# Attention in blocks: rows read and normed half a block earlier, and the sums of queries, keys and values queued from the middle of the block before

## The chip, the cores and the metric

The kernel runs on one core of one Trainium2 chip. The metric is the device time of one execution in microseconds (us), the median of several executions. Three executions before the change gave a median of 2226.68 us (2222.89 to 2229.94).

## What is computed

Two layers, one after the other, on x of 2048 rows and 640 columns. Each layer is a Fourier mixing (two matrix products along the hidden size, two along the rows) and then an attention in a sliding window of 256 rows with 32 heads of 20 columns, each behind a layer norm and each added to its input:

```
x = x + _A_ref(_layernorm(x), dft_seq_re, dft_seq_im, dft_hid_re, dft_hid_im)
x = x + _B_ref(_layernorm(x), wqkv, wo)
...
def _B_ref(x, wqkv, wo):
    H = 32; Dh = D // H; W = 256
    q, k, v = (x @ wqkv), split by heads
    scores = q k^T * Dh ** -0.5
    mask = (idx[:, None] - idx[None, :] >= 0) & (idx[:, None] - idx[None, :] < W)
    p = softmax(where(mask, scores, -1e9))
    return (p v) @ wo
```

## The kernel before

Every matrix product of two float32 operands is made as three float16 products (high x high, high x low, low x high) into one sum. The mixing stage of a layer ends with the input of the attention in DRAM (`x2_d`), 16 tiles of 128 rows. The first two tiles (block 0) are normed and turned at the end of the mixing stage; all other rows are read, normed and turned inside the attention.

**Blocks, visits, steps.** `attention` walks through 8 blocks of 256 rows. A block takes 16 visits; `now[0]` counts them in twos, so that a block runs over the steps r = 0, 2, ... 30, and "r18 of block 4" is a place in the program. A visit deals with four heads and 128 queries: `scores` (query times key, for the row maxima), 8 visits later `by_key` (the same products, turned) and `probabilities`, 11 later `values`, 12 later `back`. Per visit VectorE runs L1133 twice and L1134 twice, GpSimd runs L1188 and L1190, ScalarE L1184 twice.

**Fill.** Behind these, a visit runs one unit of fill on TensorE, mostly 15 matmuls: a sum of queries or keys (`qk`, 10 units per block: 5 of keys, then 5 of queries), of values (`v`, 4 units), or of the output projection (`out`, 4 units). `next_unit` takes the ready unit that is due first; `must` prefers those that the coming block needs, from a point that MUST_TO and FIRST_TO set. At r0 of block b, `queue_qk(b + 1)` and `queue_v(b + 1)` put the units of the next block into the fill, the sums due at r24 (QK_SLOT). `flush` forces what is left.

**From a sum to the scores.** A sum goes to `qf` (ScalarE L361) and to high and low parts in `early` (GpSimd L362, L363), and is stored to DRAM (`qkd<-early`). The store is held for one visit (`hold`). When the last of 5 sums is through, `load_stack` loads the block's keys (`ks<-qkd`) or queries (`qs<-qkd`) with six DMAs into the form that the heads need, and `ones_stack` fills the rows beside them. There are two buffers of queries and three of keys, so that the loads of block b + 1 can't start before r16 of block b (the `at` of `hold`). The row maxima go to DRAM and back (`htd<-ht`, `qs<-htd`, four visits ahead of their use).

**Rows.** At r26 of block b two tiles of block b + 3 are read from `x2_d` (L185, `x<-x2d`), at r0 of the next block `rows_norm` starts: its parts run as `slow_step`s, one or two per visit, on VectorE (L138, L141, L147 to L151, L165), then `split` on ScalarE (L176) and GpSimd (L177). `rows_turn` turns the result with a DMA transpose (L193, `early<-xs`), in layer 0 at r18, in layer 1 at r26, and marks the rows as done 6 steps later; the sums of the block wait for that mark. `new_rows`, at r14, takes the buffer for them (two in turn).

**Queues.** All these DMAs are issued by SyncE, in the order of the program (`load`, L185; `turn_load`, L193), with those of the output projection: `ot<-os` (a transpose), `x<-x2d` and `x3d<-x`. A DMA whose data isn't ready holds up all behind it. TensorE, VectorE, ScalarE and GpSimd also run in the order of the program; all matmuls are issued by L125.

Of the kernel before, what the change touches and what calls it, by code (L numbers as in the profile page):

```python
# [12 lines left out]
F16 = mybir.dt.float16  # L13
# [5 lines left out]
S, D, H, DH, P = 2048, 640, 32, 20, 128  # L19
NT = S // P  # L20
ND = D // P
# [4 lines left out]
NP = H // 2  # L26
# [8 lines left out]
FULL_TO = 244  # L35
FIRST_FILL = 2000
FILL_LAST = 8
QK_SLOT = 24
NEXT_STEPS = (10, 22)
OUT_STEPS = (4, 40, 8)  # L40
LAST_STEPS = (1, 258)
# [2 lines left out]
KEY_LAG = 8  # L44
VALUE_LAG = 11
BACK_LAG = 12
STEPS = ((1, 2), (0, 2))
MUST_TO = 24
HOLD = 2
FIRST_TO = 4  # L50
PIECES = 2
TURN_LAG = 6
UNIT = 384
# [1 line left out]
M_UP = 2.0 ** 15  # L55
SHIFT = -20.0
TURN_STEPS = 8
X2_STEP = 26
ROWS_STEP = 14
HIDDEN_STEP = 10  # L60
ROW_STEPS = 3
# [10 lines left out]
def body(ctx: ExitStack, tc: tile.TileContext, x_in, cmat, whid, wqkv, wo, out):  # L72
    nc = tc.nc
    pers = ctx.enter_context(tc.tile_pool(name="pers", bufs=1))
    keep = ctx.enter_context(tc.tile_pool(name="keep", bufs=1))
# [733 lines left out]
    def attention(layer, proj, dst, final):  # L809
        with ExitStack() as st:  # L810
# [6 lines left out]
            sb = pool("sb")  # L817
# [5 lines left out]
            fill = []  # L823
# [12 lines left out]

            def proj_qk(b, w, ct):
                if ct == 0:
                    hold(partial(ones_stack, b, w), 2 * NP * (b - 1) + 2 * KEY_LAG if b > 2 else 0)
                yield from proj.qk(b, w, ct)  # L840
                if ct == ND - 1:
                    hold(partial(load_stack, b, w), 2 * NP * (b - 1) + 2 * KEY_LAG if b > 2 else 0)

            def proj_v(b, ti, n):
                j = 2 * b + ti
# [79 lines left out]
            held = []  # L925

            def hold(f, at=0):
                held.append((max(now[0] + HOLD, at), f))

            def run_held(upto):  # L930
                for item in [h for h in held if h[0] <= upto]:
                    held.remove(item)
                    item[1]()

            proj.held = hold
            slow, idle, handed, later = deque(), deque(), deque(), []

            def new_xs():
                while len(later) > 2:
                    later.pop(0)[1]()  # L940
                return sb.tile([P, 2, D], F16, tag="xs", name="xs", bufs=3)

            def run_later():
                while later and later[0][0] <= now[0]:
                    later.pop(0)[1]()

# [16 lines left out]
            def split_wo():  # L963

                fs = [keep.tile([P, D], F32, tag="res1", name="wst", bufs=2) for n in range(2)]
                for n in range(2):
                    load(fs[n], wo[:, n])
                yield
                for n in range(ND):
                    f, sc = fs.pop(0), wsc[:, 1:2]  # L970
                    nc.scalar.activation(bo[0][:, n], f, AF.Copy, scale=sc)
                    nc.vector.scalar_tensor_tensor(bo[1][:, n], f, sc, bo[0][:, n], op0=OP.mult, op1=OP.subtract)
                    for _ in range(3):
                        yield
                    if n + 2 < ND:
                        fs.append(keep.tile([P, D], F32, tag="res1", name="wst", bufs=2))
                        load(fs[-1], wo[:, n + 2])

            def rows_norm(b, x2s):

                ys = []
                yield from norm_steps(x2s, ys)
                for t, y in enumerate(ys):
                    xs = new_xs()
                    split(xs[:, 0], xs[:, 1], y, nc.gpsimd)
                    later.append((now[0] + ROW_STEPS, partial(rows_turn, b, xs, t)))
                    yield

            def rows_turn(b, xs, t):
# [16 lines left out]
            OS, OT, X2, done = {}, {}, {}, {}  # L1006
# [3 lines left out]
            now = [0]  # L1010
# [75 lines left out]
            def flush(kind):  # L1086
                while any(u.kind == kind for u in fill) or (unit[0] and unit[0].kind == kind):
                    if unit[0] is None:
                        unit[0] = min((u for u in fill if u.kind == kind), key=lambda u: u.due)
                        fill.remove(unit[0])  # L1090
                    if step(unit[0]) is None:
                        unit[0] = None
                if kind[0] == "qk":
                    run_held(1 << 20)

            TOP, PT, topped = {}, {}, [None]

# [120 lines left out]
            def back(n):  # L1218
                b, k = divmod(n, NP // 2)
                t = PVS.pop(n)  # L1220
                pv = new_f().rearrange("p (a b) -> p a b", a=4)
                for m in range(2):
                    transpose(pv[:, 2 + m], t[:, m], idf)
                pbv = pv[:, 2:].rearrange("p m (h e) -> p (m h) e", e=32)
                if k == 0:
                    flush(("out", b - 3))
                    OS[b] = sb.tile([P, 2, 2, D], F16, tag="os", name="os", bufs=3)
                r = sb.tile([P, 8], F32, tag="r", name="r", bufs=2)
                cs = slice(4 * k * DH, 4 * (k + 1) * DH)
                o = sb.tile([P, 2, 4 * DH], F32, tag="o", name="o", bufs=2)  # L1230
                hi, lo = (OS[b][:, :, m, cs] for m in range(2))
                nc.vector.reciprocal(r, pbv[:, :, DH])
                nc.vector.tensor_tensor(o.rearrange("p m (h e) -> p (m h) e", e=DH), pbv[:, :, :DH],  # L1233
                                        r.unsqueeze(2).to_broadcast([P, 8, DH]), op=OP.mult)
                nc.gpsimd.tensor_copy(hi, o)  # L1235
                nc.gpsimd.tensor_tensor(lo, o, hi, op=OP.subtract)
                last = b == NBQ - 1
                d1 = (k + 1) * 4 * DH // P
                if last and d1 > k * 4 * DH // P and (d1 > 2 or k > LAST_FROM):
                    for m in range(2):  # L1240
                        step0 = max(now[0] + LAST_STEPS[0], NG + 2 * KEY_LAG if m else LAST_STEPS[1] if d1 < ND else 0)
                        fill.append(Unit(step0, last_out(2 * b + m, lastd[0], d1), "last", NS + 2 * d1 + m, [(2 * b + m - 2, 2)]))
                    lastd[0] = d1
                elif k == NP // 2 - 1 and not last:
                    for m in range(2):
                        i = 2 * b + m
                        at, due, kind = now[0] + OUT_STEPS[0] + OUT_STEPS[2] * m, 2 * NP * (b + 2) + OUT_STEPS[1], ("out", b)
                        need = [(i - 2, 2)] if i > 1 else []
                        outs.append((at, need, partial(out_turn, i)))
                        fill.append(Unit(at, out_tile(i), kind, due + 3 * m + 2, [(i, 1)]))  # L1250

            NBQ = S // QB

            NG = NT * NP
            NS = NG - 4 + 2 * BACK_LAG

            def queue_qk(b):
                for w in (1, 0):
                    for ct in range(ND):
                        need = [("rows", b, t) for t in range(2)] if b > 1 else []  # L1260
                        fill.append(Unit(0, proj_qk(b, w, ct), ("qk", b), 2 * NP * (b - 1) + QK_SLOT, need, ns=15 * 109))

            def queue_v(b):
                for ti in range(2):
                    for n in range(2):
                        fill.append(Unit(2 * NP * (b - 1), proj_v(b, ti, n), ("v", b), 2 * NP * b + 2 * VALUE_LAG, ns=15 * 136))

            def slow_step():
                with tc.issue_after(topped[0]):
# [17 lines left out]
            for G in range(NS // 2 + 1):  # L1287
                now[0] = g = 2 * G
                b, r = divmod(g, 2 * NP)
                if g < NG:  # L1290
                    if r == 0:
                        flush(("qk", b))
                        if b < NBQ - 1:
                            queue_qk(b + 1)
                            queue_v(b + 1)
                    scores(G)
                keyed = 0 <= G - KEY_LAG < NG // 2
                if keyed:
# [13 lines left out]
                n = due(G, BACK_LAG)  # L1312
                if n is not None:
                    back(n)
                c = b + 2 + (r > 0)
                if g < NG and c < NBQ and (g == 0 or r == X2_STEP):
                    x2s = [keep.tile([P, D], F32, tag="res0", name="x2", bufs=2) for t in range(2)]
                    for t in range(2):
                        load(x2s[t], x2_d[2 * c + t])
                if g < NG and c < NBQ and r == 0:  # L1320
                    slow.append(rows_norm(c, x2s))
                if g < NG and r == ROWS_STEP:
                    flush(("v", b))
                    if b < NBQ - 2:
                        proj.new_rows(b + 2)
                if g < NG and r == HIDDEN_STEP:
                    if b == NBQ - 1 and not final:
                        flush(("v", b))
                        hidden = Hidden(xu_d)
                        pieces = hidden.pieces()  # L1330
                        for k in range(2):
                            fill.append(Unit(g + NEXT_STEPS[k], hidden.stage(k, None), "next", NG + k))
# [4 lines left out]
                    next(pieces, None)  # L1337
                while handed and handed[0][0] <= now[0]:
                    handed.popleft()[1]()
                run_held(now[0])  # L1340
                if outs and outs[0][0] <= g and all(k in done for k in outs[0][1]):
                    outs.pop(0)[2]()
                n = due(G, VALUE_LAG)
# [46 lines left out]
```

## Time and profile before

| | us |
|---|---|
| median of three executions | 2226.68 |
| the profiled execution | 2233.76 |
| its span in the trace | 2232.0 |
| TensorE busy, all stages | 2038.7 |
| first mixing stage, 0 to 578.2 | 578.2 |
| attention of layer 0, blocks 0 to 7, 578.2 to 1097.8 | 519.6 |
| attention of layer 1, blocks 0 to 7, 1668.0 to 2181.8 | 513.8 |

The span is that of the one profiled execution, from its first to its last instruction; 1.8 us of its time lie outside. In the prediction, rows of stretches give the stretch in microseconds from the span's start, its length, and per engine (PE, PE's weight loads, VectorE, ScalarE, GpSimd) the busy time with the number of instructions, then the clock that TensorE was granted (1.00 is full), the DMA share and GB/s. Rows of a timeline give start, time, engine, line, operation, operands and, in brackets, the idle time ahead and what ended it; "SPq" is SyncE's queue.

### The profile page before, as it was taken

The page shows a single profiled execution, that of the slowest core. Times are in us where ns is not written, and L with a number is a line of the kernel's source. Part 1 is how long each engine was busy: PE and PEld are TensorE (multiplying, and loading weights), DVE is VectorE, ACT ScalarE, POOL GpSimd, SP SyncE. Part 2 cuts the span into 40 slices and gives each one's busy share as a digit, 9 for nine tenths or more (in the row PEclk, how much of TensorE's full clock was granted, in tenths as well). Part 3 has the DMA queues.
Part 4 walks back from the last instruction along what each step waited for, and adds up shares of the span by engine and source line. Part 5 has one row for each costly group of instructions (what it writes and reads, how often), then busy time and mean ns, then how long its engine had stood idle before and what let it go on. Part 6 is the DMA issues. An engine that isn't in the chain of part 4 may idle for free.

```text
span 2232.0 us, 54291 instructions
## 1 busy us (share of the span) xinstructions
PE 2038.7 (91%) x21145; PEld 1470.8 (66%) x21145; DVE 1507.8 (68%) x3253; ACT 1127.5 (51%) x1971; POOL 1448.6 (65%) x2170
## 2 busy tenths in 40 slices
PE   7999999999988998899889999999998899988987
PEld 4667666767656776666556777677675676766764
DVE  8777778676676776655538677775857676755652
ACT  5444455433255666555554444343424566655654
POOL 5667688769455777655457768676755676656643
PEclk9999999999999999999999999999999999999989
DMA  7555565474534555434436454545754334434321
GB/s 252 179 199 178 181 213 197 146 281 150 127 81 110 108 114 104 89 80 106 137 115 182 146 185 149 166 168 186 256 142 85 88 81 104 110 83 105 79 63 49
DMA packets 280502, 311.00 MB, mean 139 GB/s; under 512 B 107572, under 2 KB 214836, under 8 KB 271156
## 3 DMA queue, kind: packets, MB, share of 16 engines
q1 hardware_dynamic: 279668, 306.88, 47.3%
q8 instruction: 165, 2.70, 0.5%
q14 instruction: 93, 0.76, 0.1%
q10 hardware_dynamic: 576, 0.66, 0.1%
HBM read 201.72 MB, written 83.46 MB: 128 GB/s over the span
## 4 chain that ended last, share of the span: by engine, by line
PE 57%; DVE 16%; DMA 11%; ACT 5%; issue 4%; POOL 3%; SPq 3%; DVEq 0%; POOLq 0%; ACTq 0%
PE pf L125 26%; PE y L125 10%; PE st L125 7%; PE x L125 7%; PE z L125 6%; DVE cc L523 5%; DMA qs<-qkd 4%; DVE m L1134 3%; ACT ptq L1184 3%; SPq L185 2%; DVE st L1133 2%; DMA qkd<-early 2%; DMA ks<-qkd 2%; DMA res<-accd 1%; DVE lnt L150 1%
## 5 line engine op out<-in xcount | busy, mean ns | idle before, releaser
L125 PEld LDWEIGHTS <-cc 128*128 128x128 f16 x5376 | 525.2, 98 | 209.1 <-issue 8.2
L1184 ACT ACTIVATE ptq<-st,shift,alpha 128x768 f32<-128x768 f32 (+2 forms) x512 | 484.7, 950 | 305.8 <-PE st L125 253.0
L125 PEld LDWEIGHTS <-big 128*128 128x128 f16 x4320 | 417.9, 98 | 164.3 <-issue 62.2
L1133 DVE COPY_PREDICATED st<-mask,st 128x256 f32<-128x256 int32 x448 | 190.0, 424 | 251.9 <-PE st L125 247.3
L1134 DVE TENSOR_REDUCE m<-st 128x2 f32<-128x512 f32 (+1 forms) x512 | 342.5, 671 | 10.7 <-DVE st L1133 0.5
L125 PE MATMUL pf<-early,big 128*128 128x256 f16 x2400 | 289.8, 274 | 7.9 <-ACT ht L1151 4.3
L125 PE MATMUL pf<-big 128*128 128x320 f16 x1680 | 242.0, 302 | 28.3 <-DVE zc L283 16.7
L125 PE MATMUL y<-zc,cc 128*128 128x320 f16 x1728 | 263.4, 299 | 3.7 <-DVE pf L546 3.7
L1188 POOL TENSOR_SCALAR_AFFINE_SELECT ptq<-ptq 128x512 f32<-128x512 f32 x224 | 145.8, 651 | 155.5 <-ACT ptq L1184 155.1
L523 DVE SCALAR_TENSOR_TENSOR cc<-cs,cc 128x512 f16<-128x512 f32 x256 | 229.0, 901 | 0.0
L520 ACT ACTIVATE cc<-cs 128x512 f16<-128x512 f32 x256 | 149.1, 621 | 135.1 <-POOL cs L513 61.1
L125 PE MATMUL st<-ks,qs 62*128 62x128 f16 (+1 forms) x2016 | 131.3, 240 | 83.5 <-DMA qs<-qkd 43.7
L523 DVE SCALAR_TENSOR_TENSOR cc<-cq,cc 128x512 f16<-128x512 f32 x192 | 198.6, 1035 | 0.2 <-ACT cc L520 0.2
L1190 POOL TENSOR_SCALAR_AFFINE_SELECT ptq<-ptq 128x512 f32<-128x512 f32 x256 | 164.3, 642 | 47.0 <-ACT ptq L1184 46.4
L125 PE MATMUL pf<-ptq,v 128*32 128x128 f32 (+1 forms) x3840 | 188.2, 335 | 1.6 <-DVE early L283 1.2
L125 PEld LDWEIGHTS <-qs 62*128 62x128 f16 x2016 | 85.1, 95 | 144.3 <-issue 123.6
L125 PE MATMUL z<-zc,cc 128*128 128x320 f16 x1152 | 177.7, 299 | 2.7 <-DVE res L546 1.7
L125 PE MATMUL x<-zc,cc 128*128 128x320 f16 x1152 | 178.9, 300 | 0.0
L587 POOL TENSOR_TENSOR res<-res,pf 128x320 f32<-128x320 f32 x64 | 77.7, 1214 | 138.8 <-DVE pf L546 130.7
L1235 POOL CAST os<-o 128x160 f16<-128x160 f32 x128 | 41.8, 326 | 183.3 <-DVE o L1233 183.2
L125 PE MATMUL pf<-big,early 128*128 128x320 f16 x960 | 149.6, 311 | 1.7 <-ACT ht L1151 0.9
L125 PEld LDWEIGHTS pf<-ptq,v 128*32 128x32 f32 x3840 | 112.6, 111 | 44.1 <-issue 3.5
(135 smaller groups left out, 3364.5 us busy)
## 6 DMA issues: line engine op xcount, KB each, us to landing
cq<-in_cmat_dram SPq DMA_DIRECT2D x64, 1024.0 KB
accd<-res SPq DMA_DIRECT2D x96, 320.0 KB
res<-accd SPq DMA_DIRECT2D x96, 320.0 KB
x<-x2d SPq DMA_DIRECT2D x64, 320.0 KB
qkd<-early SPq DMA_DIRECT2D x160, 128.0 KB
ks<-qkd SPq DMA_DIRECT2D x108, 160.0 KB
qs<-qkd SPq DMA_DIRECT2D x84, 160.0 KB
x2d<-res SPq DMA_DIRECT2D x32, 320.0 KB
```

The source lines that it names most:

```text
L125: i = getattr(nc.tensor, what)(*args, **kw)
L150: ts(u, g, g, h, op0=OP.mult, op1=OP.mult)
L185: i = nc.sync.dma_start(out, in_)
L520: nc.scalar.activation(cc[m][:, 0], f, AF.Copy, scale=C_UP)
L523: nc.vector.scalar_tensor_tensor(cc[m][:, 1], f, C_UP, cc[m][:, 0], op0=OP.mult, op1=OP.subtract)
L587: nc.gpsimd.tensor_tensor(x1[:, hi], x1[:, hi], p1, op=OP.add)
L1133: nc.vector.copy_predicated(sp[:, :, 2 * P:3 * P], mask[:, None, :].to_broadcast([P, 2, P]), far)
L1134: topped[0] = nc.vector.tensor_reduce(TOP[n][:, pi, :, k], sp[:, :, c0:3 * P], axis=AX.X, op=OP.max).ins
L1184: nc.scalar.activation(o[:, pi], tps[pi][:, :, first * P:3 * P], AF.Sigmoid, bias=shift, scale=alpha[:, 0:1])
L1188: nc.gpsimd.affine_select(out=q[:, :, a0], in_=q[:, :, a0], pattern=[[0, 4], [-1, P]], base=0, channel_multiplier=1, compare_op=OP.is_gt, ...
L1190: ins = nc.gpsimd.affine_select(out=q[:, :, a0 + 2], in_=q[:, :, a0 + 2], pattern=[[0, 4], [1, P]], base=0, channel_multiplier=-1, compare ...
L1235: nc.gpsimd.tensor_copy(hi, o)
```

## The change

- `queue_qk` and `queue_v` of block b + 2 are called at r14 of block b (ROWS_STEP), behind `new_rows`; block 0 alone still queues block 1 at r0. Units of values now also wait for their rows. The sums are due at r20 (QK_SLOT, MUST_TO).
- The rows of block b + 3 are read at r12 (X2_STEP) and their norm starts at r16 of block b. `rows_turn` waits in a list of its own (`turning`) until r16 of the next block, in tiles of their own (`rx`, two); the tile `xs` of `next_norm` comes from the pool `keep`, two in turn.
- The loads of queries and keys keep their earliest place (`at`), for block 2 too; `flush` no longer runs held DMAs ahead of it, and the run at the end of a visit takes those whose time has come.
- The output units of layer 0 wait until the weights `wo` are split.

```diff
-QK_SLOT = 24
+QK_SLOT = 20
-MUST_TO = 24
+MUST_TO = 20
-FIRST_TO = 4
+FIRST_TO = 0
-X2_STEP = 26
+X2_STEP = 12
...
-                    hold(partial(ones_stack, b, w), 2 * NP * (b - 1) + 2 * KEY_LAG if b > 2 else 0)
+                    hold(partial(ones_stack, b, w), 2 * NP * (b - 1) + 2 * KEY_LAG if b > 1 else 0)
...
-                    hold(partial(load_stack, b, w), 2 * NP * (b - 1) + 2 * KEY_LAG if b > 2 else 0)
+                    hold(partial(load_stack, b, w), 2 * NP * (b - 1) + 2 * KEY_LAG if b > 1 else 0)
...
-                held.append((max(now[0] + HOLD, at), f))
+                held.append((max(now[0] + HOLD, at), f, at))
...
-                for item in [h for h in held if h[0] <= upto]:
+                for item in [h for h in held if min(h[0], max(h[2], upto)) <= now[0]]:
...
-                while len(later) > 2:
+                while len(later) > 1:
                     later.pop(0)[1]()
-                return sb.tile([P, 2, D], F16, tag="xs", name="xs", bufs=3)
+                return keep.tile([P, 2, D], F16, tag="xs", name="xs", bufs=2)
...
+                while turning and turning[0][0] <= now[0]:
+                    turning.pop(0)[1]()
...
+                    if n == ND - 1:
+                        done["wo"] = now[0]
...
-                    xs = new_xs()
+                    xs = sb.tile([P, 2, D], F16, tag="rx", name="rx", bufs=2)
                     split(xs[:, 0], xs[:, 1], y, nc.gpsimd)
-                    later.append((now[0] + ROW_STEPS, partial(rows_turn, b, xs, t)))
+                    turning.append((max(now[0] + ROW_STEPS, 2 * NP * (b - 2) + ROWS_STEP + 1), partial(rows_turn, b, xs, t)))
...
-                    run_held(1 << 20)
+                    run_held(0)
...
-                        fill.append(Unit(at, out_tile(i), kind, due + 3 * m + 2, [(i, 1)]))
+                        fill.append(Unit(at, out_tile(i), kind, due + 3 * m + 2, [(i, 1)] + ["wo"] * (layer == 0)))
...
-                        fill.append(Unit(2 * NP * (b - 1), proj_v(b, ti, n), ("v", b), 2 * NP * b + 2 * VALUE_LAG, ns=15 * 136))
+                        need = [("rows", b, ti)] if b > 1 else []
+                        fill.append(Unit(2 * NP * (b - 1), proj_v(b, ti, n), ("v", b), 2 * NP * b + 2 * VALUE_LAG, need, ns=15 * 136))
...
                     if r == 0:
                         flush(("qk", b))
-                        if b < NBQ - 1:
-                            queue_qk(b + 1)
-                            queue_v(b + 1)
+                        if b == 0:
+                            queue_qk(1)
+                            queue_v(1)
...
-                c = b + 2 + (r > 0)
+                c = 2 if g == 0 else b + 3
...
-                if g < NG and c < NBQ and r == 0:
+                if g < NG and c < NBQ and (g == 0 or r == X2_STEP + 4):
                     slow.append(rows_norm(c, x2s))
                 if g < NG and r == ROWS_STEP:
                     flush(("v", b))
                     if b < NBQ - 2:
                         proj.new_rows(b + 2)
+                        queue_qk(b + 2)
+                        queue_v(b + 2)
...
-                run_held(now[0])
+                run_held(1 << 20)
```

Two places show how instructions move. The first is SyncE in layer 0, the later half of block 4. `qkd_0_157` are the queries of block 5, `qkd_1_158` its keys, `x2d_93` and `x2d_94` the rows of block 7, `ot<-os` a transpose for the output projection, `htd` the row maxima. Before:

```order
L193 DMA_TRANSPOSE ot<-os 128x10x128
L185 DMA x_12108<-x2d_84 128x640
L185 DMA xud_129<-xs 128x1280
L185 DMA qs<-htd_163 2x512 x2
L185 DMA qkd_0_157<-early 128x2x256
L185 DMA htd_164<-ht 16x128
L185 DMA x_12252<-x2d_93 128x640
L185 DMA x_12253<-x2d_94 128x640
L185 DMA qkd_0_157<-early 128x2x256
L185 DMA qs<-qkd_0_157 20x16x256 x6
```

The same place after the change:

```order
L193 DMA_TRANSPOSE early<-rx 128x10x128 x2
L185 DMA qs<-htd_165 2x512 x2
L185 DMA ks<-onesd_169 2x4096 x2
L185 DMA ks<-qkd_1_158 20x16x256 x6
L185 DMA qs<-onesd_168 2x4096 x2
L185 DMA qkd_0_157<-early 128x2x256
L185 DMA htd_166<-ht 16x128
L185 DMA qkd_0_157<-early 128x2x256
L185 DMA res<-x3d_95 128x640
L185 DMA qs<-htd_166 2x512 x2
L185 DMA qkd_0_157<-early 128x2x256
L185 DMA qs<-qkd_0_157 20x16x256 x6
```

The output transpose and the two reads of rows no longer stand between the last stores and the load of the queries; the transposes of rows (`early<-rx`) now stand ahead of the keys' load, and the queries' load follows it within a few rows.

The second is VectorE in layer 0, where the norm of block 7's rows starts. `x_12252` and `x_11774` are the tile of these rows, before and after; L916 is the second half of an output tile. Before:

```order
L916 SCALAR_TENSOR_TENSOR x_12108<-pf,beta,x_12108 128x320
L1133 COPY_PREDICATED st_6968<-mask,st_6968 128x2x128
L1232 RECIPROCAL r<-pf 128x8
L1134 TENSOR_REDUCE m<-st_6968 128x2
L1133 COPY_PREDICATED st_6969<-mask,st_6969 128x2x128
L1233 TENSOR_TENSOR o<-pf,r 128x160
L1134 TENSOR_REDUCE m<-st_6969 128x2
L138 BN_STATS lnst<-x_12252 128x6
```

After:

```order
L1137 COPY_PREDICATED st_6968<-mask,st_6968 128x2x128
L1236 RECIPROCAL r<-pf 128x8
L1138 TENSOR_REDUCE m<-st_6968 128x2
L1137 COPY_PREDICATED st_6969<-mask,st_6969 128x2x128
L1237 TENSOR_TENSOR o<-pf,r 128x160
L1138 TENSOR_REDUCE m<-st_6969 128x2
L138 BN_STATS lnst<-x_11775 128x6
L916 SCALAR_TENSOR_TENSOR x_10644<-pf,beta,x_10644 128x320
```

The statistics of these rows move from the first visit of block 5, behind output tile 5 (`x_12108`), to the middle of block 4, ahead of the end of output tile 3 (`x_10644`); lines from L976 on have numbers higher by 2 to 7 in the changed kernel (L1133 is L1137 there, L1232 is L1236).

More of the change, by code (lines that the diff above doesn't have):

```diff
@@ L935, in attention @@
             proj.held = hold
-            slow, idle, handed, later = deque(), deque(), deque(), []
+            slow, idle, handed, later, turning = deque(), deque(), deque(), [], []
             def new_xs():
-                while len(later) > 2:
+                while len(later) > 1:
                     later.pop(0)[1]()
-                return sb.tile([P, 2, D], F16, tag="xs", name="xs", bufs=3)
+                return keep.tile([P, 2, D], F16, tag="xs", name="xs", bufs=2)
             def run_later():
+                while turning and turning[0][0] <= now[0]:
+                    turning.pop(0)[1]()
                 while later and later[0][0] <= now[0]:
```

## The prediction

> **What bounds the kernel now.** I read the chain of waits first: it tells which engine sets the end.
>
> ```profile
> PE 57%; DVE 16%; DMA 11%; ACT 5%; issue 4%; POOL 3%; SPq 3%; DVEq 0%; POOLq 0%; ACTq 0%
> PE pf L125 26%; PE y L125 10%; PE st L125 7%; PE x L125 7%; PE z L125 6%; DVE cc L523 5%; DMA qs<-qkd 4%; DVE m L1134 3%; ACT ptq L1184 3%; SPq L185 2%; DVE st L1133 2%; DMA qkd<-early 2%; DMA ks<-qkd 2%; DMA res<-accd 1%; DVE lnt L150 1%
> ```
>
> TensorE (PE) carries the end, but 4% stands on `qs<-qkd`, the load of a block's queries, and 2% on `qkd<-early`, the store of their sums. Both belong to attention, so I cut the two attention stages into their blocks. Every 32nd L1133 (two per visit, 16 visits per block) opens a block. Columns: stretch, length, busy time of each engine with its instructions, granted clock, DMA share, GB/s. The rows are blocks 1 to 6, of layer 0 and then of layer 1.
>
> ```profile
> 635.30:702.80 67.50, 55.62 (x723) 40.29 (x724) 44.38 (x108) 37.44 (x66) 39.90 (x86) 0.93 0.40 89
> 702.80:763.90 61.10, 58.32 (x857) 43.54 (x857) 49.40 (x126) 41.58 (x64) 45.20 (x99) 1.00 0.46 88
> 763.90:825.30 61.40, 58.62 (x858) 43.69 (x859) 49.73 (x126) 41.09 (x63) 45.26 (x99) 1.00 0.54 124
> 825.30:899.10 73.80, 59.24 (x857) 44.07 (x857) 47.48 (x120) 42.31 (x65) 46.45 (x100) 0.94 0.50 108
> 899.10:968.50 69.40, 64.34 (x888) 47.11 (x889) 45.01 (x109) 41.51 (x64) 43.61 (x98) 0.97 0.44 100
> 968.50:1036.50 68.00, 63.38 (x887) 46.80 (x887) 38.30 (x85) 40.37 (x62) 40.42 (x92) 0.98 0.34 80
> ...
> 1720.70:1788.20 67.50, 57.55 (x722) 40.88 (x723) 43.47 (x105) 36.34 (x64) 38.74 (x86) 0.91 0.41 89
> 1788.20:1847.80 59.60, 57.81 (x857) 43.36 (x857) 44.45 (x107) 40.95 (x63) 43.71 (x98) 1.00 0.39 85
> 1847.80:1914.10 66.30, 59.74 (x857) 44.32 (x858) 44.99 (x108) 40.52 (x62) 43.75 (x98) 0.97 0.48 106
> 1914.10:1982.90 68.80, 58.88 (x857) 43.96 (x858) 44.55 (x107) 40.84 (x63) 43.64 (x98) 0.95 0.50 113
> 1982.90:2054.90 72.00, 63.90 (x888) 47.32 (x888) 44.98 (x109) 41.49 (x64) 43.70 (x98) 0.95 0.40 86
> 2054.90:2124.90 70.00, 63.63 (x887) 47.19 (x888) 38.30 (x85) 40.38 (x62) 40.40 (x92) 0.96 0.35 78
> ```
>
> These rows carry the argument. Blocks of 857 matmuls do the same work, and last from 59.6 to 73.8 us. The shortest, block 2 of layer 1, has a clock of 1.00 and PE busy for 57.81 of its 59.60 us. So an undisturbed visit takes 59.6 / 16 = 3.73 us, and what a block has beyond that is a stall, or the lower clock around one. The waits of PE name the stalls: over 578.2 to 1097.8 us (layer 0) and then 1668 to 2182 us (layer 1); total, times, longest.
>
> ```profile
> PE st L125 <- DMA qs<-qkd: 20.4, 7, 8.4
> PE pf L125 <- DMA ot<-os: 5.4, 1, 5.4
> ```
>
> ```profile
> PE st L125 <- DMA qs<-qkd: 23.2, 8, 4.7
> PE pf L125 <- DMA early<-xs: 3.9, 2, 3.1
> PE pf L125 <- DMA ot<-os: 2.7, 1, 2.7
> ```
>
> Fifteen waits for a block's queries, 43.6 us. The longest shows how they come about: SyncE's queue in layer 0, block 4 (start, issue time), and then PE.
>
> ```profile
> 862.49 2.87 SPq L185 DMA_DIRECT2D ks<-qkd  x6
> ...
> 870.68 4.50 SPq L193 DMA_TRANSPOSE early<-xs  x2
> ...
> 884.93 0.38 SPq L185 DMA_DIRECT2D qkd<-early  x1
> 888.58 2.90 SPq L185 DMA_DIRECT2D qs<-qkd  x6
> ```
>
> ```profile
> 894.40 0.37 PE L125 MATMUL st<-ks,qs 62*128 62x256 f16 x1 [8.36 <-DMA qs<-qkd]
> 897.63 0.71 PE L125 MATMUL st<-ks,qs 62*128 62x256 f16 x8 [2.87 <-DMA qs<-qkd]
> ```
>
> SyncE issues in program order. The last store of sums left at 884.93, the load had to wait for it until 888.58, and PE, through with block 4, stood for 8.36 + 2.87 us. The query sums of block 5 end at step r24 of block 4 and their load stands at r26: three visits (11.2 us) before the block's end, for store, load and whatever SyncE has ahead of them.
>
> **The change part by part.** *Sums earlier.* The sums of block b+2 enter the fill at r14 of block b instead of r0 of block b+1. In the new order of the program a block's query sums end at r18 or r20, and the load stands at r20 or r22 (before: sums at r20 to r24, load at r22 to r26). Against the stalls: in layer 0 the load into block 5 goes from r26 to r20, three visits or 11.2 us, against a wait of 11.2 us; in layer 1 from r26 to r22, 7.5 us, against the two waits there, of which the longest is 4.7 us. The order rows shown with the change say the same of SyncE: behind block 5's last stores there is no longer a transpose of outputs or a read of rows. So I take these stalls to go whole, except the one into block 1, where the load stays at r22.
>
> I price this by blocks, as excess over the clean one. With 857 matmuls: 61.10, 61.40 and 73.80 in layer 0 against 59.60 give 1.5 + 1.8 + 14.2; 66.30 and 68.80 in layer 1 give 6.7 + 9.2, with the 3.1 us wait for rows inside the 6.7. Blocks of 888 hold two fill units of 15 matmuls more. A unit costs by its kind:
>
> ```profile
> 870.23 1.80 PE L125 MATMUL pf<-early,big 128*128 128x256 f16 x15
> ...
> 879.42 2.20 PE L125 MATMUL pf<-bo,ot 128*128 128x320 f16 x15
> ```
>
> The two extra units are of the second kind, so their clean length is 59.6 + 2 x 2.2 = 64.0, and the excess 5.4 + 4.0 in layer 0 and 8.0 + 6.0 in layer 1. These nine blocks give 56.8 us.
>
> Block 1 has no clean sister. There I count the wait for `ot<-os` (5.4 and 2.7): the output units that ran into it, at r30, now run at r8 and r0 of block 2, behind their transposes of r24. The clock around them:
>
> ```profile
> 684.00:704.00 20.00, 12.61 (x152) 8.16 (x145) 7.41 (x18) 7.14 (x11) 5.68 (x15) 0.83 0.67 147
> ...
> 1774.00:1786.00 12.00, 7.29 (x85) 4.59 (x80) 4.53 (x10) 4.67 (x7) 3.99 (x11) 0.79 1.04 191
> ```
>
> In the first, 0.17 x 20 = 3.4 us of clock are gone, some of it while PE stood anyway; I take 2.4. In the last, 0.21 x 12 = 2.5; I take 1.7. Block 1 gives 5.4 + 2.4 + 2.7 + 1.7 = 12.2. The Trainium skill ("TensorE: Matmul & The Clock Gate", Part 1) has the clock halve after an idle window of about 3.4 us. By that, the last stretch, where no wait exceeds 2.7 us, would owe nothing to the clock, and the sum would be 1.7 us less; its row with 0.79 speaks against that, and I follow the row.
>
> *Unfilled visits.* Before, no unit runs at r30 of block 0 or r28 of block 1 (r30 and r28 in layer 1 too); the change fills three of these four, and block 7 has one unit less, at r16. Work only changes places, but a visit without a unit leaves PE waiting for ScalarE; I take 4 us for both layers, bounds 0 and 3 x 2.2 = 6.6.
>
> *Rows read and normed earlier.* Per block: two reads, four statistics, two aggregates, the small steps of two rows, two norms (L165), two ScalarE and two GpSimd splits, two transposes. All of these ran before, once per block; only their places change. Their cover is the room beside PE: the fullest block, of 763.90, has VectorE at 49.73 and GpSimd at 45.26 of 61.40 us. If the cover failed, VectorE would stand in front of the row maxima that scores wait for. The read now leads its first statistic by two visits (r12 to r16, 7.5 us) instead of three. The group's row (busy, mean, idle before) shows what the old lead left:
>
> ```profile
> L138 DVE BATCH_NORM_STATS2 lnst<-x 128x6 f32<-128x320 f32 x72 | 32.6, 479 | 0.9 <-DMA x<-x2d 0.8
> ```
>
> 0.9 us over all 72 of them. One visit less costs between 0 and 3.7 us a time; I take 0, since the old waits are that small, and keep 12 x 3.7 = 44 us for the far end.
>
> *Transposes of rows at r16, used at r22* (r18 and r26 in the first block of each layer that has them). That adds a wait: PE's units of block b+2 stand behind `early<-rx`, and all later scores behind those. The lead is three visits and some 1.5 us, 12.7 us. The nearest row is a late one, in layer 1: program place r26 of block 2, about 1788.2 + 13 x 3.73 = 1836.7.
>
> ```profile
> 1837.45 3.06 SPq L185 DMA_DIRECT2D qs<-qkd  x6
> 1840.56 3.93 SPq L193 DMA_TRANSPOSE ot<-os  x1
> ...
> 1846.58 5.45 SPq L193 DMA_TRANSPOSE early<-xs  x2
> ```
>
> ```profile
> 1855.64 1.60 PE L125 MATMUL pf<-early,big 128*128 128x256 f16 x8 [3.09 <-DMA early<-xs]
> ```
>
> Here 19 us pass from the place to the landing, but the queries' load, an output transpose and a read stand ahead. From the issue it is 1855.6 - 1846.6 = 9 us, inside 12.7. At r16 SyncE has next to nothing ahead of the transposes. So I take 3 us in all, for a block in which an output transpose comes first (r14, layer 0 block 3); bounds 0 and 11 places at the late row's delay.
>
> *Queue order.* The two transposes now stand ahead of the keys' load and of the last stores: 4.5 us of issue that were behind the keys before. With the load 7.5 to 11.2 us earlier I cost it at nothing. The Trainium skill ("DMA: Bandwidth & Descriptors", § Queues, rings and completion order) says that a DMA engine consumes a ring in order. By that, data queue up as well as issues, and the first rival gains in weight; no row here separates the two.
>
> **The sum.** 56.8 + 12.2 + 4 - 3 = 70 us. The profiled execution took 2233.8 us (span 2232.0), 7 above the median of 2226.7; the stalls are its own, so the same kind of execution would take 2163.8, and I set the median at 2226.7 - 70 = **2156.7**.
>
> **The rivals.** *The load is still late at half the boundaries.* For it: 4.5 us of transposes, 2.9 of keys and the stores are now bunched between r16 and r22. Against: blocks 2 and 3 of layer 0, whose load stands at r24, show only 1.5 and 1.8 us of excess. Half of the gain: 2226.7 - 35 = 2192.
>
> *The new wait becomes the bound (slower).* If `early<-rx` came as late everywhere as in the row above, 19 us after its place, PE would stand 19 - 12.7 = 6.3 us, and about 1.7 for the clock, at 11 places: 88 us, and 2226.7 - 70 + 88 = 2245. It decides from 70 / 11 = 6.4 us per place, clock included. For it: that row. Against: what was ahead of it there isn't at r16.
>
> *The change doesn't do what it says.* If the queries' load were held by something other than the sums, say DMA traffic, blocks would stay as they are: 2222 to 2231. Against: a DMA share of 0.34 to 0.54 over these blocks, and a load that follows the last store by the store's own landing.
>
> **How the numbers follow.** Forecast 0.76, first rival 0.13, slower 0.05, no effect 0.06. About 0.3% (7 us) is what a measurement here can tell from no change. Faster: 0.76 + 0.13 = 0.89; same 0.06; slower 0.05. The range goes down to 2138, for the unknown costs at nothing, the upper bound for the unfilled visits (together 5.6 us below the forecast) and the stalls into block 1 gone as well (two waits in each layer at the mean of 43.6 / 15 = 2.9 us, 11.6 us, and a little clock), and up to 2192, the first rival, which also covers most of a read that comes late.
>
> **What would show it.** Right: blocks 2 to 4 at 59 to 61 us in both layers with a clock near 1.00; waits of PE for `qs<-qkd` down from 43.6 to under 10 us, the rest at the start of block 1; no long wait for `early<-rx`. Wrong: the same waits, only shorter (first rival); a gap of 5 us or more at r22 of every block (second); VectorE standing for `x<-x2d` (the cover of the reads). The forecast also falls if units moved into blocks 1 to 4 make their visits longer than 3.73 us.

## The result and the profile after

The changed kernel takes **2171.39 us** (median of four executions, 2165.37 to 2175.20) against 2228.31 us before (four, 2222.89 to 2233.42): a ratio of 0.9742, 95% interval 0.9710 to 0.9775. That is 57 us less; the forecast was 70 us less, 2156.7, in a range of 2138 to 2192. The profiled execution took 2171.61 us with a span of 2169.9, 62 us less than the profiled execution before.

The chain of waits after the change (the page's part 4):

```profile
PE 66%; DVE 16%; ACT 5%; DMA 5%; issue 4%; POOL 3%; SPq 0%; DVEq 0%; POOLq 0%; ACTq 0%
```

TensorE's share of the chain rose from 57% to 66%, DMA's fell from 11% to 5% and SyncE's queue from 3% to 0%. `qs<-qkd`, 4% before, is no longer in its list of lines. The waits of TensorE, over blocks 0 to 7 of layer 0 and then of layer 1 (total, times, longest):

```profile
PE st L125 <- DMA qs<-htd: 5.5, 3, 2.8
PE st L125 <- DMA qs<-qkd: 5.1, 3, 2.4
...
PE pf L125 <- DMA early<-rx: 1.4, 1, 1.4
```

```profile
PE st L125 <- DMA ks<-htd: 8.3, 3, 4.2
...
PE pf L125 <- DMA early<-rx: 1.3, 1, 1.3
```

The waits for a block's queries went from 43.6 us in 15 to 5.1 us in 3, and those for the output transposes (`ot<-os`) from 5.4 and 2.7 us to 0.4 in all. But 13.8 us of waits for the row maxima (`htd`) have come in their place (before the change there were 3.0 us of them, at most 1.1 each). The blocks show where. The same columns as in the prediction; blocks 1 to 6 of layer 0, then 0 to 6 of layer 1:

```profile
630.40:690.70 60.30, 54.98 (x738) 40.67 (x739) 47.38 (x109) 40.41 (x71) 40.07 (x84) 0.97 0.51 120
690.70:750.00 59.30, 58.12 (x857) 43.22 (x856) 45.23 (x109) 40.63 (x62) 44.20 (x99) 1.00 0.42 99
750.00:812.30 62.30, 58.85 (x857) 43.61 (x858) 50.45 (x132) 42.20 (x65) 48.12 (x105) 1.00 0.52 117
812.30:879.60 67.30, 59.29 (x857) 43.89 (x857) 47.19 (x120) 41.81 (x64) 45.28 (x99) 0.99 0.46 104
879.60:943.30 63.70, 62.80 (x887) 46.56 (x888) 41.56 (x96) 41.00 (x63) 40.91 (x95) 0.98 0.52 117
943.30:1005.40 62.10, 60.94 (x873) 44.70 (x873) 39.05 (x86) 39.77 (x60) 38.33 (x89) 1.00 0.43 89
...
1640.00:1700.60 60.60, 47.70 (x437) 32.35 (x436) 38.76 (x98) 21.40 (x46) 25.40 (x58) 0.92 0.41 89
1700.60:1761.40 60.80, 55.94 (x738) 41.47 (x739) 45.82 (x121) 37.00 (x66) 39.77 (x89) 0.94 0.45 91
1761.40:1820.20 58.80, 57.39 (x858) 43.37 (x857) 44.82 (x109) 40.58 (x62) 44.56 (x101) 1.00 0.45 107
1820.20:1879.10 58.90, 57.89 (x858) 43.45 (x857) 44.45 (x109) 41.17 (x63) 43.63 (x100) 1.00 0.49 112
1879.10:1939.80 60.70, 59.66 (x873) 44.68 (x871) 44.41 (x109) 41.60 (x64) 43.55 (x99) 1.00 0.48 110
1939.80:2002.40 62.60, 61.65 (x887) 46.06 (x886) 39.81 (x87) 41.60 (x64) 43.50 (x99) 1.00 0.47 106
2002.40:2064.00 61.60, 60.79 (x872) 44.65 (x872) 39.01 (x85) 39.78 (x60) 38.34 (x89) 1.00 0.46 87
```

Blocks 2 to 6 of layer 1 have a clock of 1.00 and TensorE busy for all but 0.8 to 1.4 us of each. Two rows stand out. Block 4 of layer 0 still takes 67.3 us, 8 more than block 2 with the same 857 matmuls. And block 0 of layer 1 takes 60.6 us; before the change it took 51.1:

```profile
1669.60:1720.70 51.10, 44.34 (x437) 31.27 (x436) 37.76 (x93) 21.05 (x46) 26.36 (x58) 0.99 0.45 96
```

In both, SyncE's queue tells why (start, issue time). Layer 1, block 0:

```profile
1655.27 0.32 SPq L185 DMA_DIRECT2D htd<-ht  x1
1669.20 0.85 SPq L185 DMA_DIRECT2D x<-x2d  x2
1670.15 0.59 SPq L185 DMA_DIRECT2D ks<-htd  x2
```

For 13.9 us SyncE issued nothing, then the read of rows that the change put at r12. What it waited for, over 1650 to 1690 us:

```profile
SPq L185 <- DVE lny L165: 13.2, 1, 13.2
```

L165 is the last instruction that reads the rows of block 2. Those lie in the two `res0` tiles into which the rows of block 3 are to be read. In layer 1 the norm gets two `slow_step`s in every second visit (in layer 0 one and two in turn) and reaches L165 only at 1668.29 us. All behind the read waits with it, the row maxima (`ks<-htd`) first, and after them TensorE, which is ready for `by_key`:

```profile
1672.93 0.55 PE L125 MATMUL st<-ks 62*128 62x128 f16 x4 [4.24 <-DMA ks<-htd]
...
1683.80 0.67 PE L125 MATMUL st<-ks 62*128 62x128 f16 x4 [2.81 <-DMA ks<-htd]
```

Layer 0, block 4, the same with another load:

```profile
850.83 0.38 SPq L185 DMA_DIRECT2D qkd<-early  x1
863.04 0.34 SPq L185 DMA_DIRECT2D res<-x3d  x1
863.48 0.55 SPq L185 DMA_DIRECT2D qs<-htd  x2
864.13 0.38 SPq L185 DMA_DIRECT2D qkd<-early  x1
866.54 3.07 SPq L185 DMA_DIRECT2D qs<-qkd  x6
```

`res<-x3d` loads the residual of the second mixing stage. It goes into `res0` as well, and since the last rows now leave `res0` half a block earlier, this load has moved in SyncE's order from block 5 into block 4, ahead of the last store and the load of block 5's queries. SyncE issued nothing for 12 us before it; what it waited for, over 840 to 881 us:

```profile
SPq L185 <- DVE lnt L151: 10.8, 1, 10.8
```

This L151 runs right behind the first L165 of block 7's rows (862.10 to 863.02 us on VectorE), which frees the tile. TensorE paid behind it, over 860 to 880 us:

```profile
PE st L125 <- DMA qs<-htd: 4.3, 2, 2.8
PE st L125 <- DMA qs<-qkd: 2.4, 1, 2.4
```

### The profile page after: what moved, and what is told of

It reads as the page before. It is cut to its first block, busy times and chain, and to the rows that moved or that the text cites. A ratio compares the mean times of both kernels' runs of the same rounds, so it can differ in the third digit from the quotient of the medians.

```text
span 2169.9 us, 54390 instructions
## 1 busy us (share of the span) xinstructions
PE 2025.3 (93%) x21145; PEld 1464.2 (67%) x21145; DVE 1506.9 (69%) x3253; ACT 1129.0 (52%) x1971; POOL 1448.4 (67%) x2170
## 4 chain that ended last, share of the span: by engine, by line
PE 66%; DVE 16%; ACT 5%; DMA 5%; issue 4%; POOL 3%; SPq 0%; DVEq 0%; POOLq 0%; ACTq 0%
PE pf L125 33%; PE y L125 11%; PE st L125 9%; PE x L125 7%; PE z L125 7%; DVE cc L523 5%; ACT ptq L1188 3%; DVE m L1138 3%; DVE st L1137 2%; DMA res<-accd 1%; DVE lnt L150 1%; DMA htd<-ht 1%; DVE res L546 1%; DVE lnt L151 1%; DVE lnst L138 1%
## 5 line engine op out<-in xcount | busy, mean ns | idle before, releaser
L125 PEld LDWEIGHTS <-big 128*128 128x128 f16 x4320 | 418.3, 99 | 167.0 <-issue 62.1
L1137 DVE COPY_PREDICATED st<-mask,st 128x256 f32<-128x256 int32 x448 | 190.1, 424 | 209.2 <-PE st L125 204.0
L125 PE MATMUL pf<-big 128*128 128x320 f16 x1680 | 243.0, 302 | 27.8 <-DVE zc L283 16.7
L125 PE MATMUL pf<-big,early 128*128 128x320 f16 x960 | 143.1, 302 | 1.0 <-ACT ht L1155 0.7
L125 PEld LDWEIGHTS <-ks 62*128 62x128 f16 x3008 | 108.9, 95 | 43.7 <-issue 42.6
```

Source lines behind the costliest of these rows:

```text
L125: i = getattr(nc.tensor, what)(*args, **kw)
L1137: nc.vector.copy_predicated(sp[:, :, 2 * P:3 * P], mask[:, None, :].to_broadcast([P, 2, P]), far)
```

## The experiments

Two theories stood against each other. **Mine:** the gain comes from the earlier place of the queries' load, and what is missing from the forecast are these two stalls of SyncE. **Rivals:** the gain comes from a queue cleared of reads and transposes near a block's end, whatever the place of the load; and the two waits of SyncE are a symptom, TensorE being held by VectorE or by the crowd of transfers. Ratios are to the kernel before on the same chip. The 95% interval of e1 just touches that of the changed kernel (0.9710 to 0.9775), and those of e2, e3 and e7 overlap with it, so there the lengths of single blocks and the waits say more than the times; each is from one profiled execution.

**e1, both stalls taken away.** The rows get two tiles of their own, and layer 1 reads and norms block 3's rows 10 steps later in block 0.

```diff
-                if g < NG and c < NBQ and (g == 0 or r == X2_STEP):
+                if g < NG and c < NBQ and (g == 0 or r == X2_STEP + 10 * (layer == 1 and b == 0)):
-                    x2s = [keep.tile([P, D], F32, tag="res0", name="x2", bufs=2) for t in range(2)]
+                    x2s = [sb.tile([P, D], F32, tag="x2r", name="x2", bufs=2) for t in range(2)]
...
-                if g < NG and c < NBQ and (g == 0 or r == X2_STEP + 4):
+                if g < NG and c < NBQ and (g == 0 or r == X2_STEP + 4 + 10 * (layer == 1 and b == 0)):
```

> The rows read from x2d get two tiles of their own (before they shared res0 with the residual of the next mixing stage), and in layer 1 block 0 their read and norm come 10 steps later. Theory (the 13 us that the prediction is off are two new stalls of SyncE: a read or a residual load that stands in its queue until VectorE's L165 frees a tile): both stalls go, layer 1 block 0 falls from 60.6 to about 51 to 53 us, layer 0 block 4 from 67.3 to about 60, and the time from 2171 to 2153 to 2158. Rival (SyncE's wait is harmless there; PE waits since VectorE or the queue of transfers is full with the earlier norm): 2165 to 2175.

Measured: 2152.24 us, ratio 0.9679 (0.9643 to 0.9715). Block 4 of layer 0 and block 0 of layer 1:

```profile
812.30:871.60 59.30, 58.14 (x857) 43.35 (x858) 47.02 (x119) 41.65 (x64) 43.77 (x95) 1.00 0.48 109
1630.00:1680.00 50.00, 43.71 (x437) 30.82 (x436) 39.80 (x98) 21.07 (x46) 26.40 (x58) 1.00 0.45 105
```

67.3 became 59.3 and 60.6 became 50.0, with the same matmuls and VectorE about as busy as in the changed kernel: 18.6 us in these two blocks, and 19 between the medians. This is the fastest median of the study.

**e2, only the later read** (the first and last lines of that diff).

> Only the later read in layer 1 block 0 (step 22 instead of 12); tiles as in the changed kernel. Theory: layer 1 block 0 falls to 51 to 53 us, layer 0 block 4 stays near 67; time 2161 to 2165. Rival (the wait there is for VectorE's work, not for the read in the queue): block 0 of layer 1 stays at 58 to 61 and the time at 2168 to 2175.

Measured: 2162.64 us, ratio 0.9710 (0.9685 to 0.9735).

```profile
814.60:881.70 67.10, 59.17 (x857) 43.80 (x857) 47.10 (x120) 41.76 (x64) 45.29 (x99) 0.99 0.46 106
1640.10:1688.80 48.70, 44.01 (x438) 30.97 (x436) 39.78 (x99) 21.32 (x47) 26.21 (x58) 1.00 0.49 106
```

Block 0 of layer 1 lost its stall, block 4 of layer 0 kept its own. The read in the queue was the cause, not the work on VectorE, which is the same.

**e3, only the own tiles** (the middle line).

> Only the own tiles for the rows; the read in layer 1 block 0 stays at step 12, behind the norm that holds the two tiles. Theory: layer 0 block 4 falls to about 60 us, unless the residual load, now free of the rows' tiles and earlier in the queue, waits for the store that it reads; layer 1 block 0 stays near 60; time 2162 to 2167. Rival (the residual load was not what held the queue): block 4 stays at 66 to 68 and the time at 2168 to 2175.

Measured: 2163.48 us, ratio 0.9716 (0.9693 to 0.9739).

```profile
815.40:874.70 59.30, 58.13 (x858) 43.33 (x858) 47.04 (x120) 41.65 (x64) 43.84 (x96) 1.00 0.46 109
1632.00:1692.80 60.80, 49.24 (x438) 33.15 (x436) 38.71 (x99) 21.62 (x47) 25.31 (x57) 0.89 0.38 87
```

The mirror image. The gains over the changed kernel, 8.8 and 7.9 us, add up to 16.7 by medians, against 19.2 for both. The lengths repeat: block 4 took 67.3 and 67.1 us with its stall, 59.3 and 59.3 without; block 0 took 60.6 and 60.8 with, 50.0 and 48.7 without.

**e4, only the earlier rows.** Sums queued and due as before the change. Everything else of the change stays, also its new rules for held loads and for the output units of layer 0, so "the rows part" below holds these too.

```diff
-QK_SLOT = 20
+QK_SLOT = 24
-MUST_TO = 20
+MUST_TO = 24
-FIRST_TO = 0
+FIRST_TO = 4
...
-                        if b == 0:
-                            queue_qk(1)
-                            queue_v(1)
+                        if b < NBQ - 1:
+                            queue_qk(b + 1)
+                            queue_v(b + 1)
...
-                        queue_qk(b + 2)
-                        queue_v(b + 2)
```

> Only the part that reads, norms and turns rows earlier; the sums are queued at step 0 of the block before, due at 24, as in the kernel before, and the load of the queries stands at steps 24 to 26 again. Theory (the gain comes from the earlier place of the load): the waits for qs<-qkd come back at 30 us or more and the time is 2215 to 2240. Rival (the gain comes from SyncE's queue, freed of reads, row transposes and output transposes in the later half of a block): most waits stay away and the time is 2170 to 2195.

Measured: 2210.41 us, ratio 0.9927 (0.9903 to 0.9950), between the two expectations and nearer to mine. The waits for the queries (20.0 in layer 0, 9.8 in layer 1, 29.8 us in 14) fell from 43.6 but did not go. So the rival has a share: with reads and transposes out of the later half of a block, the load, at its old place, costs less waiting.

**e5, only the load put late.** The changed kernel with the load of the queries held to r28, which is later than any place before the change (r22 to r26).

```diff
-                    hold(partial(load_stack, b, w), 2 * NP * (b - 1) + 2 * KEY_LAG if b > 1 else 0)
+                    hold(partial(load_stack, b, w), 2 * NP * (b - 1) + (2 * KEY_LAG if w else 28) if b > 1 else 0)
```

> The changed kernel with the load of a block's queries held back to step 28 (from 20 or 22), for blocks 2 to 7 of both layers; sums, stores and rows stay. Theory (the place of the load decides, two visits or 7.5 us from its place to the block's end against some 8 to 10 us from issue to landing): a wait of 2 to 5 us for qs<-qkd at 12 block starts, with the lower clock 3 to 6 us each, and 2205 to 2245. Rival (the sums' earlier end alone does it, the load has room): 2165 to 2180.

Measured: 2238.40 us, ratio 1.0022 (1.0001 to 1.0042). The whole gain is gone, with all sums as early as in the changed kernel. The waits in the two layers:

```profile
PE st L125 <- DMA qs<-qkd: 28.4, 10, 3.6
```

```profile
PE st L125 <- DMA qs<-qkd: 20.3, 9, 3.9
```

48.7 us of waits, where the changed kernel has 5.1, cost 2.8% (1.0022 - 0.9742), 62 us: more than the 43.6 us of added waits. The clock is lower too (0.975 on average, 0.986 in the changed kernel), which fits; how the rest divides was not measured.

**e6, only the due places back.** The changed kernel with QK_SLOT, MUST_TO and FIRST_TO as before (24, 24, 4); the load then stands at r24 in all blocks.

> The changed kernel with the due places of before (24, and 20 in the first block); sums are still queued half a block earlier, the load stands at step 24 in all blocks. Theory (four visits, 15 us, are enough for store and load when nothing else stands between): blocks 2 to 6 lose 0 to 2 us each, 2168 to 2190; what decides is the queueing in the middle of the block. Rival (the due place, that is step 20 instead of 24, is what made the stalls go): half of the stalls come back, 2195 to 2215.

Measured: 2177.84 us, ratio 0.9742 (0.9709 to 0.9776), the ratio of the changed kernel. Three blocks lose more than the 2 us that I allowed: block 6 of layer 0 (67.7 us against 62.1) and of layer 1 (66.0 against 61.6), each with one unit of fill more, and block 3 of layer 1 (62.3 against 58.9); blocks 3 and 5 of layer 0 are 2 us shorter than in the changed kernel, block 5 with one unit less. The waits for the queries are 9.9 us in five, against 5.1 in three. Four visits from the load to the block's end are mostly enough.

e4 and e6 differ only in when the sums are queued, and in no due place: 0.9927 there, 0.9742 here. So it is the queueing in the middle of the block that makes the load early enough, and not the earlier due place.

**e7, a short lead for the rows.** Rows marked as done one visit after their transposes are queued.

```diff
-                done["rows", b, t] = now[0] + TURN_LAG
+                done["rows", b, t] = now[0] + 2
```

> The changed kernel with the rows marked as done one visit after their transposes are queued instead of three, so that sums stand at step 18 or 20 behind transposes of step 16. It prices the added wait for early<-rx, which the prediction took to be covered by 12.7 us of lead with some 9 us needed. Theory: a lead of one or two visits is 5 to 9 us, PE waits 0 to 5 us at up to 11 places where a sum of the next block is taken at once, 2175 to 2215. Rival (the due order keeps those sums behind others anyway, or the transposes land at once): 2165 to 2175.

Measured: 2186.02 us, ratio 0.9791 (0.9763 to 0.9819). TensorE waits for `early<-rx` 6.8 us in layer 0 and 8.8 in layer 1, in three waits:

```profile
618.07 3.36 PE L125 MATMUL pf<-early,big 128*128 128x256 f16 x15 [6.79 <-DMA early<-rx]
```

```profile
1707.52 3.36 PE L125 MATMUL pf<-early,big 128*128 128x256 f16 x15 [5.00 <-DMA early<-rx]
...
1755.82 3.06 PE L125 MATMUL pf<-early,big 128*128 128x256 f16 x15 [3.83 <-DMA early<-rx]
```

The two visits that were taken away are the cover; with them, the waits are 1.4 and 1.3 us. Only three of the 11 places show it. That units of the running block are due first elsewhere, as the rival has it, would explain this; no run shows it.

**e8, the rows-only kernel without the two stalls** (the edits of e1 on e4).

> The rows-only kernel (rows early, sums and load of queries as in the kernel before) with the own tiles and the later read of layer 1 block 0. Theory (the two stalls of SyncE come with the earlier read of rows, and have nothing to do with the sums): layer 1 block 0 falls from 59.9 to about 50 us, layer 0 block 4 from 71.6 to about 65, and the time from 2210 to 2191 to 2198; the rows part would then be worth some 35 us by itself and the sums part the rest. Rival (the stalls belong to the crowd of both parts): 2204 to 2212.

Measured: 2201.15 us, ratio 0.9870 (0.9847 to 0.9893), between the two expectations.

```profile
821.60:889.90 68.30, 60.92 (x872) 45.52 (x872) 50.91 (x132) 42.64 (x66) 46.94 (x100) 0.98 0.52 114
1662.80:1711.70 48.90, 44.15 (x440) 31.08 (x438) 39.75 (x98) 21.34 (x47) 26.30 (x57) 1.00 0.47 109
```

Block 0 of layer 1 went from 59.9 to 48.9 us as expected: that stall belongs to the early read alone. Block 4 of layer 0 went from 71.6 only to 68.3, since the load of block 5's queries is late there with or without the stall (6.8 us of waits at its end in e4, 5.0 in e8); it also holds one unit of fill more than in e1 (872 matmuls). So the rows part is worth about 1.3% (29 us), the sums part, on top of it and with both stalls gone, 3.2 - 1.3 = 1.9% (some 43 us).

## Why the prediction was right, and where it was off

- **The bound and the main term.** The stalls at block ends were what could be had, and the place of the queries' load was the lever. e5 moves nothing else and loses the whole gain, though to a place later than the old ones; e4 against e6 shows the same for the old places. "I take these stalls to go whole" was nearly so: 43.6 us of waits became 5.1, of them 2.0 at the start of block 1, as foreseen, and 0.7 and 2.4 into blocks 4 and 5 of layer 0. Blocks 2 to 4 were to last 59 to 61 us: in layer 1 they took 58.8 to 60.7, but in layer 0 59.3, 62.3 and 67.3.
- **The price by blocks.** The nine blocks priced at 56.8 us fell, after less before, by 1.8, -0.9, 6.5, 5.7 and 5.9 in layer 0 and 7.4, 8.1, 9.4 and 8.4 in layer 1: 52.3 us. Three of them are short of their price: block 3 (1.8) and block 4 (14.2) of layer 0 and block 4 of layer 1 (9.2, with one unit of fill more than before). Block 3 still has waits of 1.3 us for row maxima and 0.7 for queries. With the stall in block 4 of layer 0 taken away (8.0 us in e1) the sum is 60.3. Block 1 was priced at 12.2 and fell by 7.2 + 6.7 = 13.9.
- **What the sum left out.** Four more blocks (0 and 7 of layer 0, 2 and 7 of layer 1) fell by 5.9 us together. In block 0 of layer 0 a wait of 3.4 us, put down to a load of the weights (`wst<-in_wo_dram`), is gone, with 2.0 for queries in its place; no term stood for it. Block 0 of layer 1 grew by 9.5. All sixteen blocks: 52.3 + 13.9 + 5.9 - 9.5 = 62.6 us, where the spans differ by 62.1.
- **The last step of the sum.** The 70 us were read in an execution of 2233.8 us and taken from a median of 2226.7, though the text itself says that the stalls are that execution's own. Profile against profile the change brought 62 us, median against median 57: 5 of the 13 us that are missing come from this step. The lower end of the range counts four waits of 2.9 us into block 1; the trace before has one, of 2.0 us in layer 1.
- **The step that failed** is the one on rows read earlier: "I take 0, since the old waits are that small". I asked how long before its first use a read is issued, and not how long after its place it can be: its tile was still held by the rows before it. So I priced a late read at VectorE, where the changed kernel has no wait for it (0.0 us before all 72 of L138), while it stood in SyncE's queue, ahead of row maxima, stores and the queries' load. The place was in the code (`res0`, two tiles, one norm at a time), and the order of SyncE shows `res<-x3d` among the rows that I printed. Measured, the two stalls cost 14 us by the ratios (0.9742 - 0.9679 = 0.6%) and 19 by the medians; without them the change brings 71 us (ratio of e1) to 76 (its median), where 70 were forecast.
- **The added wait.** 3 us taken, 2.7 measured (1.4 + 1.3), and e7 shows that the lead was needed: two visits less brought 12.9 us more of these waits. The time rose by 0.5% (0.9791 - 0.9742), 11 us.
- **Unfilled visits** (4 us) weren't tested by themselves.
- **The rivals.** The first (half the boundaries still late) was right in kind for one boundary, from block 4 to block 5 of layer 0, though from a tile and not from the bunched transposes. The slower one did not come. That the change does nothing is refuted by the result.

## What to carry to other kernels

When a load is moved ahead, look for the moment its destination comes free, not only for the moment its data are wanted: in a queue that issues in order, a load that waits for a tile holds up everything behind it, and the engine that pays is another one. Price a stall at a stage's edge by setting the disturbed stage beside an undisturbed one of the same work; here that held within a few microseconds, clock included. And a place in the program is worth most where its lead just falls short: here a lead of two visits for the queries' load lost the whole gain (e5), and one of four kept it (e6).

## What the hardware showed that was not expected

A small store right behind six large loads was late to land. In the changed kernel the store of the row maxima behind the six loads of queries took 6.35 us (the chain at the end of block 3, layer 0), and one behind the six loads of keys 5.89 us (layer 1, block 0):

```profile
803.45 6.35 DMA htd<-ht
...
1676.58 5.89 DMA htd<-ht
```

On the second hangs the second wait of TensorE there, 2.81 us for `ks<-htd`: the loads of keys and this store both stood behind the stalled read. In a quiet stretch of the kernel before, the load that waits for such a store follows 1.4 us behind it:

```profile
829.73 0.31 SPq L185 DMA_DIRECT2D htd<-ht  x1
831.13 0.54 SPq L185 DMA_DIRECT2D qs<-htd  x2
```

The Trainium skill ("DMA: Bandwidth & Descriptors", § Queues, rings and completion order) has each DMA engine consume its ring in order; the 6.35 us are in keeping with that. No experiment here moved that store by itself, so that the loads ahead of it are the cause is argued and not shown.
